# One parking transfer per pair of blocks, another order of queries, and a new plan, in a fused attention and state-space kernel

## The chip, the cores and the metric

The kernel runs on one core of a Trainium2 chip. A core has five engines that run their own instruction streams side by side and meet through semaphores: PE (matmuls), ACT (activation functions), DVE (vector operations), POOL (vector operations on SBUF) and SP, which here issues nearly all DMA transfers. SBUF is the working memory, 128 partitions wide; PSUM is the small memory into which PE writes. The metric is the device time of one execution in microseconds (us); less is better.

## What is computed

One layer has two branches over the same input x (2048 positions, 512 channels) and a gate between them. Cut to what matters:

```python
g = sigmoid((x * gate_w).sum(-1, keepdims=True))
q, k, v = split(x @ wqkv)                  # 32 heads of 16 channels
p = softmax(einsum("bhqd,bhkd->bhqk", q, k) * 16 ** -0.5)
a = einsum("bhqk,bhkd->bhqd", p, v).reshape(1, 2048, 512) @ wo
K = einsum("dn,dnl,dn->dl", C, exp(dt * A * l), dt * B).real   # 128 states
b = causal_convolution(x, K) + x * Dskip   # written with an FFT of length 4096
return g * a + (1 - g) * b
```

Nearly all the time goes to the softmax: 32 heads times 2048 x 2048 scores, each needing an exponential.

## The kernel before

**Attention.** The scores are cut into *tiles* of 128 keys by 512 queries. Four heads that lie in four strips of 32 partitions are worked on together; their four tiles for the same 128 keys are a *quad*. Sixteen quads (all 2048 keys) make a *block*: one set of four heads against 512 queries. There are 32 blocks, so 512 quads and 2048 tiles. Block `b` has the query chunk `qc = b // 8` and the head set `b % 8`; two blocks that follow each other (`b` even and odd) share a *pair* of channels and end up in one tile `ON`.

For three tiles at a time (a *group*, 683 of them) PE writes scores into one of two PSUM buffers `SC` (`qk`), and ACT turns them into exponentials in the ring `ET` (`ex`, line 1027), which has `NS` slots of one tile, and from group `NSG` on `NS2` slots, the further ones named `EX`. PE then multiplies a quad of exponentials with the values `VE` and adds them up in the PSUM buffer `OA` (`pv`), whose columns are the 512 queries of the block. All of these run through one helper, so all matmuls show as line 760.

**Quads given to DVE and POOL.** So that ACT needs fewer exponentials, some quads are taken from it. For such a quad, four groups in a row give their third tile to DVE, so that ACT does two tiles a group instead of three. DVE turns the score into an integer whose bits, read as bf16, are about the exponential (`bits`, line 1049, tile `DZ`). POOL makes three shifted copies by an integer addition over the whole quad (line 1068, tile `DU`; line 1064 is the same on DVE for the last groups), and PE multiplies all four versions with the values (`sums`), four sets of four matmuls instead of one set. The mean of the four has a small error.

**The other branch.** DVE builds powers and tables for the state-space kernel in four quarters (`bases`, `tables`: tiles `Z`, `B`, `T`), PE makes convolution taps from them (`kstage`, PSUM buffer `MB`), the taps go to HBM and come back as `H`, the input as `U`, and PE convolves them (`ystage`, 32 steps, MB<-U,H). Projections, the gate and the output product run in between, all through the one buffer `MB`.

**End of a block.** `norm_a` (line 1089) transposes `OA` in squares of 32 by 32 into `OT`, so that the queries lie on partitions; `norm_b` takes the reciprocal of the sums (1097), multiplies in the gate `gq` for `qc >= 2` (1100), and multiplies out into `ON` (1106). For the first `SPILL = 3` query chunks, `ON` of a pair is *parked* in HBM (`gm_od`, line 1823, in `norms`) and later comes back by a transposing DMA as `OnR` (line 1702, in `outs`); for the last chunk `norm_c` transposes it on the spot.

**Order of queries.** Projections place Q through `ROWS` and `TURNED` (line 861, and line 1895 for the first one): of each 128 queries, position 8 t + r holds query 16 r + t. The outputs leave for HBM in the same order (`out_dma`).

**What sets the order.** A planner in the kernel's own Python code, with a cost per instruction, writes out each engine's stream. `Sched.fill` picks pieces of side work (projections, tables, convolution, output) until the modelled time at which ACT ends a group plus `OVER` (two values: for a group with a tile on DVE, and without). `decide` chooses which quads go to DVE: it needs a free `DZ` buffer (`WIN`: group range, number of `DZ`, number of `DU`), modelled idle time on DVE (`DVCAP`), and fewer quads so far than the table `PACE` allows at that group (pairs of group and quads, straight lines between them). A quad may also lie across two blocks between the groups `STRX` and `STRE`. Where PE would otherwise have too little to do, it gets filler matmuls on a zero tile `wm`; `FILL` and `LOW` (from group 260 on) say how much. `GATE`, `BG0` to `BG3`, `XGO` say from which point on side work may start. DMA transfers with `pace` are issued only when the modelled queue of transfers is short enough (`BACK`), and follow ACT's groups through a semaphore. `LAZY`, `PDEL`, `OUTP`, `TP`, `KP` and `REST` set priorities; `US` sets the numbers of `U` buffers.

Of the kernel before, what the change touches and what calls it, by code (L numbers as in the profile page):

```python
# [12 lines left out]
ALU = mybir.AluOpType  # L13

P = 128
S = 2048
D = 512
NH = 32
DH = 16
T = 16  # L20
R8 = P // T
# [9 lines left out]
NDSEM = 56  # L31
ZCOL = .216 / 512
VLD = .0545
LAZY = 5
PDEL = 0.43
ZEND = 260
OUTP = 3.78
YSEG = 2
KSEG = 4
FILL = 1450  # L40
LOW = 1200
SURP = 192
FILL2 = 1500
OVER = (0.27, 0.64)
REST = (13, 1, 1792, 425)
DLAG = .6
PLAG = .4
TURN = dict(F=.105, R=.105, C=.105, H=.06)
# [5 lines left out]
VC = .065  # L54
ZLAG = .6
BARE = 2
NS = 20
NS2 = 24
NSG = 395
LATE = (5, 3)  # L60
XS = 128 * DH ** -.5 / math.log(2)
CUTS = (26, 56, 94)
XB = 128 * (127 - math.log2(5.3794))
WIN = ((0, 480, 2, 4), (480, 679, 4, 6))
PACE = ((0, 0), (61, 0), (78, 0.0), (149, 0.0), (206, 12.77), (270, 23.66), (340, 38.94), (414, 52.88), (500, 77.45), (564, 96.69), (630, 111.83), (683, 119.39))
DVEND = 679
YLP = 2
YQ = 0
XGO = 'g19'
YGO = 'projs'  # L70
YLGO = 'K14'
GATE = 'g100'
BG0 = 'g25'
BG1 = 'g20'
BG2 = 'K3'
BG3 = 'K3'
TP = 0.86
KP = 0.85
NB = 2
NT = 2  # L80
TB = 4
DIGITS = ("L16", "L64", "L80")
TM = (3,)
NZ = 2
US = [2, 12, 3]
HS = [4, 44, 8]
BACK = 0.66
UN4 = 4
HN = 1
UB = 1.10  # L90
# [3 lines left out]
OB = 0.49  # L94
# [7 lines left out]
WARM0 = 7  # L102
NN = 128
SPILL = 3
DVCAP = 8.7
DVK = 14
JS = ((2, 0, 3, 1), (1, 0, 2, 3), (0, 2, 1, 3))
FREE = 'u{}.2'
DVL = 16
STRX = 460  # L110
STRE = 640
STRK = (13, 14, 15)
VW = 136
VG = 4 * VW + 16
ROWS = [[P, 4], [R8, T], [1, R8]]
TURNED = [[P, 4], [1, T], [T, R8]]
ONES = struct.unpack("<f", bytes.fromhex("803f803f"))[0]


# [625 lines left out]
def record(nc, p, B, ins):  # L745
    KT, Qm, VE, ET, OT, ON, Rz = (B[n] for n in ("KT", "Qm", "VE", "ET", "OT", "ON", "Rz"))
    OnT = {3: B["OnT3"]}
    OA, MB = B["OA"], B["MB"]
    SC = [B["SC0"], B["SC1"]]
    sch = Sched(p)  # L750
    op, dma = p.op, p.dma
# [64 lines left out]
    for k in range(7):  # L816
        n = 1 << k
# [268 lines left out]

    def norm_a(b):
        w = b % 2
        op("DVE", lambda v: v.transpose(OT(512 * w, [[1, 512]]), OA(0, [[1, 512]])), [(OA, 0, b)], [(OT, w, b)], c=.64)  # L1089

    def norm_b(b, n, mul=True):
        w = b % 2 + 1 - n
        R = [(OT, x, b - b % 2 + x) for x in range(w, w + n)]
        K = range(w, w + n)
        qc = b // 8
        yield ("DVE", .3, 1)
        op("DVE", lambda v: v.reciprocal(Rz(16 * w, [[16, n], [1, 16]]), OT(512 * w + 16, [[512, n], [32, 16]])), R, [(Rz, x) for x in K], c=.22 + .02 * n, lk=False)
        if qc >= 2:
            yield ("DVE", .2, 1)
            op("DVE", lambda v: v.tensor_tensor(Rz(16 * w, [[16, n], [4, 4], [1, 4]]), Rz(16 * w, [[16, n], [4, 4], [1, 4]]),  # L1100
                                                B["gq"](4 * (qc - 2), [[0, n], [1, 4], [8, 4]]), ALU.mult),
               [(Rz, x) for x in K] + [(B["gq"], j) for j in range(4)], [(Rz, x) for x in K], c=.12)
        if not mul:
            return
        yield ("DVE", .6, 1)
        op("DVE", lambda v: v.tensor_tensor(ON(16 * w, [[16, n], [32, 16], [1, 16]]), OT(512 * w, [[512, n], [32, 16], [1, 16]]),
                                            Rz(16 * w, [[16, n], [1, 16], [0, 16]]), ALU.mult), R + [(Rz, x) for x in K], [(ON, x) for x in K], c=.07 + .27 * n)
# [518 lines left out]
    def gate():  # L1626
        gp, ge, g, g1, gwT, gl = (B[n] for n in ("gp", "ge", "g", "g1", "gwT", "gl"))
        yield ("AFTER", "V1.3")
        yield ("LOCK", "MB")
        for q4 in range(4):  # L1630
            yield ("PE", MM)
            for c in range(4):
                mm(lambda c=c: MB(0, [[1, 512]], 32 * c, 32), lambda q4=q4: gwT(32 * q4, [[1, 32]]),
                   lambda c=c, q4=q4: xT(q4 * S + 512 * c, [[1, 512]]),
                   [xk(k, q4) for k in range(4)] + [(gwT, 0), (gwT, 1)], [(MB, 0, 'gate')], q4 == 0, q4 == 3, pos=(0, 32 * c), c=MM if c == 0 else 0, a=128, cfg="C")
        yield ("DVE", .7, -1)
        op("DVE", lambda v: v.tensor_copy(gl(0, [[4, P], [1, 4]]), MB(0, [[1, P], [P, 4]])), [(MB, 0, 'gate')], key("gl"), c=.62)
        sch.unlock("MB")
        for c in range(4):
            yield ("SP", .6)  # L1640
            dma("SP", lambda e, c=c: e.dma_start(B["gld"].dram(4 * c, [[16, P], [1, 4]]), gl(0, [[4, P], [1, 4]], 32 * c, 1)), key("gl"), [(B["gld"], c)], c=.6, lat=2.5)
        yield ("SP", .6)
        dma("SP", lambda e: e.dma_start(gp(0, [[1, 16]]), B["gld"].dram(0, [[16, T], [16 * T, R8], [1, 16]])), [(B["gld"], c) for c in range(4)], key("gp"), c=.6, lat=2.5)
        yield ("AFTER", GATE)
        yield ("ACT", .3)
        op("ACT", lambda a: a.activation(ge(0, [[1, 16]]), gp(0, [[1, 16]]), AF.Exp, scale=-1.0), key("gp"), key("ge"), c=.2)  # L1646
        yield ("POOL", .4)
        op("POOL", lambda v: v.memset(B["gt"](0, [[1, NC]]), 0.0), [], [(B["gt"], j) for j in range(8)], c=.3)
        yield ("DVE", .4)
        op("DVE", lambda v: v.tensor_scalar(gp(0, [[1, 16]]), ge(0, [[1, 16]]), 1.0, None, ALU.add), key("ge"), key("gp"), c=.17)  # L1650
        op("DVE", lambda v: v.reciprocal(g(0, [[1, 16]]), gp(0, [[1, 16]])), key("gp"), key("g"), c=.25)
        op("DVE", lambda v: v.tensor_scalar(g1(0, [[1, 16]]), g(0, [[1, 16]]), -1.0, 1.0, ALU.mult, ALU.add), key("g"), key("g1"), c=.17)
        yield ("SP", .6)
        dma("SP", lambda e: e.dma_start(B["gd"].dram(0, [[16, P], [1, 16]]), g1(0, [[1, 16]])), key("g1"), [(B["gd"], 0)], c=.6, lat=2.5)
        for j in range(4):
            yield ("SP", .6)
            dma("SP", lambda e, j=j: e.dma_start(alt("gt", [[16, R8], [1, 16]], 32 * j), B["gd"].dram(0, [[16 * R8, T], [16, R8], [1, 16]])),
                [(B["gd"], 0)], [(B["gt"], j)], c=.6, lat=2.5)
            yield ("SP", .6)
            dma("SP", lambda e, j=j: e.dma_start(alt("gt", [[16, R8], [1, 8]], 32 * j + 1), B["gd"].dram(8, [[16 * R8, T], [16, R8], [1, 8]])),  # L1660
                [(B["gd"], 0)], [(B["gt"], 4 + j)], c=.6, lat=2.5)
        sch.mark("gt")
        yield ("SP", .6)
        dma("SP", lambda e: e.dma_start(B["gg"].dram(0, [[16, P], [1, 16]]), g(0, [[1, 16]])), key("g"), [(B["gg"], 0)], c=.6, lat=2.5)
        for j in range(4):
            yield ("SP", .6)
            dma("SP", lambda e, j=j: e.dma_start(B["gq"](0, [[8, 4], [1, 8]], 32 * j, 32), B["gg"].dram(8, [[16, 32], [512, 4], [1, 8]])),
                [(B["gg"], 0)], [(B["gq"], j)], c=.6, lat=2.5)
        sch.mark("gq")

    fo, Wo = B["fo"], B["Wo"]
# [18 lines left out]
    def outs():  # L1690
# [6 lines left out]
        for k in range(SPILL):  # L1697
            for pi in range(4):
                yield ("AFTER", f"od{k}.{pi}")
            for r in range(4):  # L1700
                yield ("SP", 1.35)
                dma("SP", lambda e, k=k, r=r: e.dma_start_transpose(B[f"OnR{k}"](128 * r, [[512, 4], [1, 128]]), B["od"].dram(512 * D * k + 128 * r * D, [[D, 128], [1, D]])),
                    [(B["od"], (k, pi, j)) for pi in range(4) for j in range(4)], [(B[f"OnR{k}"], r)], c=1.35, lat=3, b=1.3, pace=True)
        yield ("AFTER", "gt")
        for blk in range(NBLK):
            yield ("AFTER", f"yr{blk}")
# [28 lines left out]
    o, z, w = SC[(NG - 2) % 2], SC[(NG - 1) % 2], D // 2  # L1735
# [73 lines left out]
    def norms():  # L1809
        for b in range(31):  # L1810
            yield ("AFTER", f"ob{b}")
            yield ("DVE", .75, -2)
            norm_a(b)
            sch.mark(f"n{b}")
            if b == 30:
                yield from norm_b(b, 1)
            if b % 2 == 1:
                yield from norm_b(b, 2)
                k, pi = b // 8, (b % 8) // 2
                if k < SPILL:  # L1820
                    for j in range(4):
                        yield ("SP", .6, 3)
                        dma("SP", lambda e, k=k, pi=pi, j=j: e.dma_start(B["od"].dram(512 * D * k + P * pi + 32 * j, [[D, 32], [32 * D, 16], [1, 32]]), ON(0, [[32, 16], [1, 32]], 32 * j, 32)),
                            [(ON, 0), (ON, 1)], [(B["od"], (k, pi, j))], c=.57, lat=4, b=OB, pace=True)
                    sch.mark(f"od{k}.{pi}")
                else:
                    yield ("DVE", .7, 1)
                    norm_c(b)
# [92 lines left out]
    for g in range(NG):  # L1921
# [13 lines left out]
        if g + 1 < NG:  # L1935
# [5 lines left out]
            while lack >= 256 and bare:  # L1941
                n = 512 if lack >= 512 else 256
# [21 lines left out]
        while lack >= 256 and p.tm["PE"] < t + over and g < NG - 1:  # L1964
# [4 lines left out]
            n = 512 if lack >= 512 else 256  # L1969
# [67 lines left out]
```

## Time and profile before

| what | us |
|---|---|
| median of three runs | 746.74 (744.98 to 746.99) |
| the profiled execution | 746.18 |
| its span, first to last instruction | 744.3 |
| first exponential on ACT starts | 10.83 |
| parking transfers | 48, of 32 KB |

A profile shows one execution. Its span is a little shorter than the execution's time; what lies around it (1.9 us here) is not in the trace. The busy time of an engine is the time in which an instruction of its own ran; semaphores, branches and the issue of transfers don't count. The *chain that ended last* is followed back from the last instruction to whatever released each step. A row of a view gives line, engine, operation, output and input tiles with their shapes, the count, then the busy time and the mean in ns, then how long the engine had stood idle before such instructions and what ended it. "Issue" means that the engine waited for nothing that the profile shows.

### The profile page before, as it was taken

What the parts mean: (1) busy time and instruction counts of PE and PEld (TensorE: products, weight loads), DVE (VectorE), ACT (ScalarE), POOL (GpSimd) and SP (SyncE); (2) the same over time, 40 slices, a digit from 0 to 9 for tenths busy, and PEclk for the clock granted to TensorE, in tenths of its full rate; (3) what the DMA queues carried; (4) which work ended last, traced back from release to release, by engine and by line L of the source; (5) the groups of instructions that cost most, each with busy time, mean ns of one, the idle gap of its engine ahead of it and who ended that gap; (6) DMA issues with size and microseconds to landing.
All of it is one profiled execution on the core that took longest, in us unless ns stands there. A gap on an engine that the chain in (4) does not pass through costs nothing.

```text
span 744.3 us, 31873 instructions
## 1 busy us (share of the span) xinstructions
PE 692.2 (93%) x14173; PEld 299.0 (40%) x14173; DVE 659.3 (89%) x1109; ACT 728.8 (98%) x696; POOL 362.1 (49%) x365
## 2 busy tenths in 40 slices
PE   8888788888899999999999989999999999999997
PEld 4332333334444444444455444544443442222222
DVE  6999999999999999988999987977888888898886
ACT  7999999999999999999999989999999999999995
POOL 3000000000026465647545655577888888888783
PEclk9999999999999999999999999999999999999999
DMA  9556931324666755315789774478566741001001
GB/s 221 149 114 158 179 44 41 76 47 127 161 170 180 185 154 148 111 31 155 200 219 232 199 215 130 103 164 201 155 174 146 202 113 30 19 20 27 20 15 37
DMA packets 167182, 94.36 MB, mean 127 GB/s; under 512 B 107330, under 2 KB 148484, under 8 KB 167044
## 3 DMA queue, kind: packets, MB, share of 16 engines
q1 hardware_dynamic: 166084, 91.47, 50.0%
q8 instruction: 111, 1.82, 1.0%
q10 hardware_dynamic: 960, 0.85, 0.4%
q14 instruction: 27, 0.22, 0.1%
HBM read 63.42 MB, written 18.90 MB: 111 GB/s over the span
## 4 chain that ended last, share of the span: by engine, by line
ACT 91%; PE 8%; DVE 0%; issue 0%; DVEq 0%
ACT ET L1027 86%; ACT EX L1027 5%; PE SC L760 3%; PE OA L760 3%; PE MB L760 2%; DVE Qm L1895 0%; DVE VE L870 0%; DVE fo L1996 0%; DVEq L722 0%; DVE wm L814 0%; DVE KT L1898 0%; ACT ge L1646 0%; DVE idf L815 0%; DVEq L386 0%
## 5 line engine op out<-in xcount | busy, mean ns | idle before, releaser
L1027 ACT ACTIVATE ET<-SC 128x1024 bf16<-128x1024 f32 (+1 forms) x636 | 684.5, 1335 | 4.2 <-PE SC L760 4.0
L1068 POOL INT64_ADD DU<-DZ x345 | 354.6, 1042 | 344.5 <-PE MB L760 184.9
L1049 DVE TENSOR_SCALAR DZ<-SC 128x512 uint16<-128x512 f32 x464 | 310.6, 685 | 58.9 <-PE SC L760 54.9
L760 PE MATMUL SC<-Qm,KT 32*128 32x512 bf16 x2048 | 272.8, 386 | 10.6 <-ACT ET L1027 6.2
L760 PE MATMUL OA<-ET,VE 128*32 128x512 bf16 x1489 | 155.0, 389 | 30.6 <-ACT ET L1027 29.4
L760 PEld LDWEIGHTS SC<-Qm,KT 32*128 32x128 bf16 x2048 | 69.1, 91 | 193.7 <-ACT ET L1027 124.8
L760 PE MATMUL OA<-DU,VE 128*32 128x512 bf16 x1392 | 134.2, 387 | 0.6 <-POOL DU L1068 0.5
L760 PEld LDWEIGHTS MB<-U,H 128*32 128x32 bf16 x4096 | 91.3, 143 | 32.2 <-issue 15.6
L760 PE MATMUL MB<-U,H 128*32 128x128 bf16 (+7 forms) x4096 | 97.4, 224 | 2.0 <-issue 1.9
L760 PEld LDWEIGHTS OA<-ET,VE 128*32 128x32 bf16 x1489 | 40.0, 95 | 98.1 <-ACT ET L1027 54.1
L760 PE MATMUL OA<-wm 128*32 128x256 bf16 (+3 forms) x550 | 75.1, 343 | 1.2 <-DVE idf L815 1.2
L1121 DVE TENSOR_TENSOR T<-B,DT 128x1536 bf16<-128x1536 bf16 x64 | 59.6, 972 | 0.0
L760 PEld LDWEIGHTS OA<-DU,VE 128*32 128x32 bf16 x1392 | 35.5, 95 | 48.6 <-issue 40.3
L1027 ACT ACTIVATE EX<-SC 128x1024 bf16<-128x1024 f32 (+1 forms) x47 | 51.0, 1219 | 0.0
L760 PEld LDWEIGHTS MB<-T,Z 128*32 128x32 bf16 x2048 | 41.7, 156 | 12.2 <-issue 10.2
L760 PE MATMUL MB<-T,Z 128*32 128x64 bf16 (+1 forms) x2048 | 46.2, 236 | 0.0
L760 PE MATMUL OA<-DZ,VE 128*32 128x512 bf16 x464 | 45.8, 385 | 0.0
L1121 DVE TENSOR_TENSOR ft<-Z 128x512 f32<-128x512 f32 (+3 forms) x48 | 38.3, 820 | 0.3
L1121 DVE TENSOR_TENSOR Z<-ft,ft 128x1024 bf16<-128x1024 bf16 (+3 forms) x56 | 33.8, 604 | 0.5
L1602 DVE TENSOR_TENSOR Yst<-MB,gt 128x512 bf16<-128x512 f32 x32 | 21.8, 681 | 3.8 <-PE MB L760 3.8
L760 PEld LDWEIGHTS OA<-wm 128*32 128x32 bf16 (+2 forms) x550 | 20.8, 96 | 10.3 <-issue 7.0
L1089 DVE STREAM_TRANSPOSE OT<-OA 128x512 f32<-128x512 f32 x32 | 22.7, 710 | 2.0 <-PE OA L760 2.0
(143 smaller groups left out, 411.2 us busy)
## 6 DMA issues: line engine op xcount, KB each, us to landing
H<-gm_kd SPq DMA_DIRECT2D x128, 256.0 KB, 4.1
U<-gm_xs SPq DMA_DIRECT2D x128, 134.2 KB, 3.7
T<-B SPq DMA_DIRECT2D x16, 256.0 KB, 2.7
gm_yd<-Yst SPq DMA_DIRECT2D x16, 256.0 KB, 3.2
gm_kd<-Ks SPq DMA_DIRECT2D x64, 40.0 KB, 2.2
gm_xs<-xP SPq DMA_DIRECT2D x16, 136.0 KB, 5.8
gm_pd<-L SPq DMA_DIRECT2D x8, 256.0 KB, 4.3
Z<-gm_pd SPq DMA_DIRECT2D x8, 256.0 KB, 3.7
```

The costliest lines, as they stand in the source:

```text
L760: op("PE", lambda t: t.matmul(out(), lhsT(), rhs(), start=start, stop=stop, skip_group_check=True, **kw), R, W, c=c, lat=.15, a=a, cfg=cfg)
L1027: op("ACT", lambda a: a.activation(E(at, [[1, 512 * n]]), sc(0, [[1, 512 * n]]), AF.Exp, scale=DH ** -0.5), [(sc, i, g) for i in range(n)] ...
L1049: op("DVE", lambda v: v.tensor_scalar(z.u16(512 * k, [[1, 512]]), sc(1024, [[1, 512]]), XS, XB, ALU.mult, ALU.add), [(sc, 2, g)], [(z, k, ...
L1068: op("POOL", lambda v, u=u, cut=cut: v.int64_add(u.u64(), z.u64(), cut * 0x0001000100010001), R, [(u, 0, i)], c=1.016, lat=.09, lk=True)
L1089: op("DVE", lambda v: v.transpose(OT(512 * w, [[1, 512]]), OA(0, [[1, 512]])), [(OA, 0, b)], [(OT, w, b)], c=.64)
L1121: op(eng, lambda v: v.tensor_tensor(o(), a(), b_(), f), R, W, c=c)
L1602: op("DVE", lambda v, w=w, h=h: v.tensor_tensor(Yst(1024 * w + 4 * h, [[128, R8], [8, 16], [1, 4]]), MB(0, [[1, R8], [R8, 16], [NC, 4]]), ...
```

## The change

Parking becomes one transfer of 128 KB a pair of blocks instead of four of 32 KB. One transfer can only walk the partitions in their order, so row `16 p + a` of the parked chunk now holds what lies on partition `p` of its strip in square `a`. For this, `norm_a` reads `OA` in other steps (`BACKS`: one pattern for the parked chunks, one for the last), and the copies that place Q use other `ROWS` and `TURNED`: of each 128 queries, position 64 s + m now holds query 2 m + s. Sizes and counts of these instructions stay. The gate `gq` is stored in one order for the third chunk and in another for the fourth, and loaded with eight transfers instead of four. The transposing loads now wait for one parking transfer a pair.

Around this the planner's numbers are new; the description of the change says that two quads more go to DVE and POOL.

```diff
-LAZY = 5
-PDEL = 0.43
+LAZY = 4
+PDEL = 0.45
-OUTP = 3.78
+OUTP = 4.02
-FILL = 1450
-LOW = 1200
+FILL = 1500
+LOW = 1300
-OVER = (0.27, 0.64)
-REST = (13, 1, 1792, 425)
+OVER = (0.37, 0.82)
+REST = (12, 0, 1792, 475)
-NS = 20
+NS = 18
-NSG = 395
+NSG = 305
-WIN = ((0, 480, 2, 4), (480, 679, 4, 6))
-PACE = ((0, 0), (61, 0), (78, 0.0), (149, 0.0), (206, 12.77), (270, 23.66), (340, 38.94), (414, 52.88), (500, 77.45), (564, 96.69), (630, 111.83), (683, 119.39))
+WIN = ((0, 560, 3, 4), (560, 679, 4, 6))
+PACE = ((0, 0), (61, 0), (78, 0), (149, 0.0), (206, 12.24), (270, 23.13), (346, 36.66), (426, 58.37), (500, 81.91), (564, 97.72), (630, 116.08), (683, 123.09))
-XGO = 'g19'
+XGO = 'g34'
-BG0 = 'g25'
-BG1 = 'g20'
-BG2 = 'K3'
-BG3 = 'K3'
+BG0 = 'g20'
+BG1 = 'g0'
+BG2 = 'K4'
+BG3 = 'K6'
-KP = 0.85
+KP = 0.48
-US = [2, 12, 3]
+US = [2, 13, 3]
-BACK = 0.66
+BACK = 0.53
-DVCAP = 8.7
+DVCAP = 8.45
-STRX = 460
-STRE = 640
+STRX = 470
+STRE = 660
-ROWS = [[P, 4], [R8, T], [1, R8]]
-TURNED = [[P, 4], [1, T], [T, R8]]
+ROWS = [[P, 4], [64, 2], [1, 64]]
+TURNED = [[P, 4], [1, 2], [2, 64]]
+BACKS = ([[8, 16], [P, 4], [1, 8]], [[P, 4], [1, 8], [8, 16]])
...
-        op("DVE", lambda v: v.transpose(OT(512 * w, [[1, 512]]), OA(0, [[1, 512]])), [(OA, 0, b)], [(OT, w, b)], c=.64)
+        op("DVE", lambda v: v.transpose(OT(512 * w, [[1, 512]]), OA(0, BACKS[b // 8 >= SPILL])), [(OA, 0, b)], [(OT, w, b)], c=.64)
...
-                                                B["gq"](4 * (qc - 2), [[0, n], [1, 4], [8, 4]]), ALU.mult),
+                                                B["gq"](16 * (qc - 2), [[0, n], [1, 4], [4, 4]] if qc > 2 else [[0, n], [4, 4], [1, 4]]), ALU.mult),
...
-            dma("SP", lambda e, j=j: e.dma_start(B["gq"](0, [[8, 4], [1, 8]], 32 * j, 32), B["gg"].dram(8, [[16, 32], [512, 4], [1, 8]])),
+            dma("SP", lambda e, j=j: e.dma_start(B["gq"](0, [[1, 16]], 32 * j, 32), B["gg"].dram(8, [[1, 4], [16, P]]), allow_slow_non_contiguous=True),
+                [(B["gg"], 0)], [(B["gq"], (2, j))], c=.6, lat=2.5)
+            yield ("SP", .6)
+            dma("SP", lambda e, j=j: e.dma_start(B["gq"](16, [[4, 4], [1, 4]], 32 * j, 32), B["gg"].dram(12, [[16, 32], [512, 4], [1, 4]])),
...
-                    [(B["od"], (k, pi, j)) for pi in range(4) for j in range(4)], [(B[f"OnR{k}"], r)], c=1.35, lat=3, b=1.3, pace=True)
+                    [(B["od"], (k, pi)) for pi in range(4)], [(B[f"OnR{k}"], r)], c=1.35, lat=3, b=1.3, pace=True)
...
-                    for j in range(4):
-                        yield ("SP", .6, 3)
-                        dma("SP", lambda e, k=k, pi=pi, j=j: e.dma_start(B["od"].dram(512 * D * k + P * pi + 32 * j, [[D, 32], [32 * D, 16], [1, 32]]), ON(0, [[32, 16], [1, 32]], 32 * j, 32)),
-                            [(ON, 0), (ON, 1)], [(B["od"], (k, pi, j))], c=.57, lat=4, b=OB, pace=True)
+                    yield ("SP", .6, 3)
+                    dma("SP", lambda e, k=k, pi=pi: e.dma_start(B["od"].dram(512 * D * k + P * pi, [[32, 4], [D, 512], [1, 32]]), ON(0, [[32, 16], [1, 32]])),
+                        [(ON, 0), (ON, 1)], [(B["od"], (k, pi))], c=.6, lat=5, b=4 * OB, pace=True)
```

More of the change, by code (lines that the diff above doesn't have):

```diff
@@ L1100, in norm_b @@
             op("DVE", lambda v: v.tensor_tensor(Rz(16 * w, [[16, n], [4, 4], [1, 4]]), Rz(16 * w, [[16, n], [4, 4], [1, 4]]),
-                                                B["gq"](4 * (qc - 2), [[0, n], [1, 4], [8, 4]]), ALU.mult),
-               [(Rz, x) for x in K] + [(B["gq"], j) for j in range(4)], [(Rz, x) for x in K], c=.12)
+                                                B["gq"](16 * (qc - 2), [[0, n], [1, 4], [4, 4]] if qc > 2 else [[0, n], [4, 4], [1, 4]]), ALU.mult),
+               [(Rz, x) for x in K] + [(B["gq"], (qc, j)) for j in range(4)], [(Rz, x) for x in K], c=.12)
         if not mul:
@@ L1666, in gate @@
             yield ("SP", .6)
-            dma("SP", lambda e, j=j: e.dma_start(B["gq"](0, [[8, 4], [1, 8]], 32 * j, 32), B["gg"].dram(8, [[16, 32], [512, 4], [1, 8]])),
-                [(B["gg"], 0)], [(B["gq"], j)], c=.6, lat=2.5)
+            dma("SP", lambda e, j=j: e.dma_start(B["gq"](0, [[1, 16]], 32 * j, 32), B["gg"].dram(8, [[1, 4], [16, P]]), allow_slow_non_contiguous=True),
+                [(B["gg"], 0)], [(B["gq"], (2, j))], c=.6, lat=2.5)
+            yield ("SP", .6)
+            dma("SP", lambda e, j=j: e.dma_start(B["gq"](16, [[4, 4], [1, 4]], 32 * j, 32), B["gg"].dram(12, [[16, 32], [512, 4], [1, 4]])),
+                [(B["gg"], 0)], [(B["gq"], (3, j))], c=.6, lat=2.5)
         sch.mark("gq")
```

## The prediction

> **What bounds the kernel now.** I read the page's busy shares and its chain first, then the chain in order of time, then the windows.
>
> ```profile
> span 744.3 us, 31873 instructions
> ...
> PE 692.2 (93%) x14173; PEld 299.0 (40%) x14173; DVE 659.3 (89%) x1109; ACT 728.8 (98%) x696; POOL 362.1 (49%) x365
> ...
> ACT 91%; PE 8%; DVE 0%; issue 0%; DVEq 0%
> ```
>
> ACT is busy nearly always and carries 91% of the chain that ended last. What it does there is one kind of instruction, the exponential of two or three score tiles (the chain's longest pieces, out of its pieces in order of time: start, length, what):
>
> ```profile
> 17.34 130.41 ACT ET L1027 x97
> ...
> 549.30 9.17 ACT ET L1027 x10
> ...
> 718.95 0.55 PE OA L760 x8
> 719.49 0.37 PE SC L760 x3
> ```
>
> Early on all groups have three tiles: 130.41 / 97 = 1.344 us each. Late all have two, the third tile going to DVE: 9.17 / 10 = 0.917 us each. One tile less on ACT is thus worth 1.344 - 0.917 = 0.427 us, if ACT never waits. From 715 us on the chain runs through PE in steps of 0.55 + 0.37 = 0.92 us, the same beat: there PE and ACT are equally late.
>
> ```profile
> ACT ET L1027 <- PE SC L760: 4.0, 6, 1.7
> ```
>
> That is the row of ACT's waits for its scores: 4.0 us in six waits, the longest 1.7. Where they lie:
>
> ```profile
> 350.00:400.00 50.00, 48.45 (x1127) 24.22 (x1119) 45.95 (x73) 50.00 (x50) 28.51 (x29) 1.00 0.78 207
> 400.00:450.00 50.00, 46.98 (x1073) 22.85 (x1074) 44.39 (x65) 47.42 (x47) 27.72 (x27) 0.97 0.83 221
> 450.00:500.00 50.00, 49.40 (x1157) 24.34 (x1157) 40.33 (x67) 49.89 (x51) 30.84 (x30) 1.00 0.52 119
> 500.00:550.00 50.00, 49.39 (x1073) 23.28 (x1070) 41.72 (x70) 50.00 (x54) 38.04 (x38) 1.00 0.72 188
> ```
>
> and finer, around one place:
>
> ```profile
> 425.00:432.00 7.00, 4.59 (x157) 3.11 (x157) 4.90 (x6) 5.81 (x5) 1.92 (x2) 1.00 0.99 243
> 432.00:437.00 5.00, 5.00 (x69) 1.59 (x63) 4.06 (x6) 3.61 (x4) 2.06 (x2) 0.66 0.40 116
> ```
>
> Columns: length, busy time of PE, PEld, DVE, ACT, POOL, granted clock, DMA share, GB/s. ACT loses 50.00 - 47.42 = 2.58 us between 400 and 450, and the timeline shows the cause:
>
> ```profile
> 431.62 0.49 PE L760 MATMUL MB<-U,H 128*32 128x104 bf16 x18 [1.93 <-issue]
> ...
> 432.49 1.94 ACT L1027 ACTIVATE ET<-SC 128x1024 bf16<-128x1024 f32 x2 [1.68 <-PE SC L760]
> ```
>
> PE stood 1.93 us for "issue", so for nothing that the kernel waits on, while the DMA share was 0.99; ACT then starved 1.68 us. Afterwards the clock was low: 0.66 over 5 us, which is 0.34 x 5 / 0.5 = 3.4 us at half speed. The page's queue list shows what PE can have waited for without a semaphore:
>
> ```profile
> q8 instruction: 111, 1.82, 1.0%
> ```
>
> 111 blocks of 1.82 MB / 111 = 16.4 KB come by DMA beside the data. I read the hole as such a block of PE's own instructions held up by full DMA engines. That one hole is a matter of where transfers happen to lie, and any new plan redraws it.
>
> **The change, part by part.**
>
> *Two quads more.* The planner gives chosen key tiles ("quads": four score tiles) to DVE and POOL. Rows:
>
> ```profile
> L1068 POOL INT64_ADD DU<-DZ x345 | 354.6, 1042 | 344.5 <-PE MB L760 184.9
> L1049 DVE TENSOR_SCALAR DZ<-SC 128x512 uint16<-128x512 f32 x464 | 310.6, 685 | 58.9 <-PE SC L760 54.9
> ```
>
> 464 tiles are 116 quads. The diff holds no count; I take its words, 118, so eight tiles leave ACT: 8 x 0.427 = **3.42 us less on ACT**. The table PACE supports it: it caps the quads started by a given group, and at group 426 the cap rises from 52.88 + 12/86 x 24.57 = 56.3 to 58.37, while at group 275 it falls from 23.66 + 5/70 x 15.28 = 24.75 to 23.13 + 5/76 x 13.53 = 24.02. So quads move from early to middle, and the middle gains.
>
> What the other engines pay. DVE: 8 x 0.685 = 5.5 us, against 744.3 - 659.3 = 85 us idle. POOL: 6 x 1.04 = 6.3 us, half idle. PE: a quad takes 16 value matmuls instead of 4; in the chain's row above eight take 0.55 us, so four 0.28: 2 x 3 x 0.28 = 1.7 us. Where will they go?
>
> ```profile
> 450.00:500.00 50.00, 3.96 (x40) 1.07 (x40) 26.54 (x40) 30.84 (x30) 1.00 0.52 119
> 500.00:550.00 50.00, 4.89 (x52) 1.38 (x52) 34.44 (x53) 38.04 (x38) 1.00 0.72 188
> ```
>
> These are the windows for tile DZ alone (here PE, PEld, DVE, POOL). From 500 us nearly every group already gives a tile to DVE (53 for 54 of ACT's instructions); before it, 40 for 51. Room is only before 500, and the caps point to 350 to 500 us: at groups 275 and 423, which ACT reaches up to 10 us before these times (counting its instructions), they are 55.45 - 24.75 = 30.7 quads apart before and 57.56 - 24.02 = 33.5 after (at 423: 52.88 + 9/86 x 24.57 and 36.66 + 77/80 x 21.71). A cap is no count, but I take 2.8 more there: 2.8 x 4 x 0.685 = 7.7 us of DVE in windows where DVE idles 4.05 + 5.61 + 9.67 = 19.3 us, and 2.8 x 3 x 0.28 = 2.4 us of PE. PE's cover there is filler, matmuls on zeros (tile wm):
>
> ```profile
> 350.00:400.00 50.00, 1.75 (x24) 0.64 (x24) 0.00 (x0) 1.00 0.78 207
> 400.00:450.00 50.00, 2.76 (x40) 0.78 (x40) 0.00 (x0) 0.97 0.83 221
> 450.00:500.00 50.00, 1.40 (x20) 0.51 (x20) 0.00 (x0) 1.00 0.52 119
> ```
>
> That is 5.9 us. PE also idles 150 - 144.83 = 5.2 us in the three rows, 1.9 of them in the hole: 9.2 us of cover. Against it stand 2.4 us of new work and 2.8 x 4 x 0.427 = 4.8 us less time: 7.2. The cover holds with 2.0 us left, so PE's part is 0; without it PE sets the beat there and every us of PE work costs one.
>
> *Parking.* Four transfers of 32 KB become one of 128 KB, in runs of 64 bytes as before, so the engines carry the same packets.
>
> ```profile
> L1823 SPq DMA_DIRECT2D gm_od<-ON x48: 315/486/1102, 78.6 to 590.8; - x48
> ...
> gm_od<-ON SPq DMA_DIRECT2D x48, 32.0 KB, 2.7
> ```
>
> SP issues 36 fewer: 36 x 0.486 = 17.5 us saved if one long issue costs what a short one does, 0 if it costs as four. A landing takes between 2.7 us, as one of the four does, and 4 x 2.7 = 10.8 us. Nobody waits for either: ON is overwritten by the next pair, (590.8 - 78.6) / 11 = 47 us later on average, and SP is not on the chain. Cost 0, except that the loads queued behind it on SP move up by the 1.5 us of three issues and can crowd.
>
> *Order of queries.* The steps change in the transpose L1089 and in the two copies that place Q; counts and sizes don't.
>
> ```profile
> L1089 DVE STREAM_TRANSPOSE OT<-OA 128x512 f32<-128x512 f32 x32 | 22.7, 710 | 2.0 <-PE OA L760 2.0
> ...
> L861 DVE CAST Qs<-MB 128x512 bf16<-128x512 f32 x15 | 10.3, 689 | 0.8 <-PE MB L760 0.6
> L861 DVE CAST KT<-MB 128x512 bf16<-128x512 f32 x15 | 10.3, 686 | 0.7 <-PE MB L760 0.6
> ```
>
> Strided Qs and straight KT cost the same (689 and 686 ns), so steps out of PSUM are free there; a strided transpose has no row. Lower end 0; upper end one pass more, 32 x 0.71 = 22.7 us of DVE, inside its 85 us idle. I take 0, by Qs. The gates gq come in eight transfers instead of four, half of them element by element:
>
> ```profile
> L1100 DVE TENSOR_TENSOR Rz<-Rz,gq x9: 190/419/847, 463.6 to 737.2; 128x32 f32<-128x32 f32 x7, 128x16 f32<-128x16 f32 x2
> L1667 SPq DMA_DIRECT2D gq<-gm_gg x4: 432/432/458, 163.7 to 165.1; - x4
> ```
>
> From the issue at 165 us to the first reader at 463.6 lie 298 us, so 0.
>
> *Slack.* OVER lets PE's planned side work run past ACT's tick by 0.37 and 0.82 us instead of 0.27 and 0.64. Between nothing and 0.10 to 0.18 us a group lies the price; only six waits of ACT speak for room, so 0. FILL and LOW ask for 3% and 8% more side work a group; on 5.9 us of filler that is 0.5 us at most, within the 2.0 left. The other numbers of the plan (LAZY, BACK, BG0 to BG3, US, STRX and the like) shift work and add none: 0, their risk stands in C and D. The ring ET of 18 slots instead of 20 (24 from group 305) costs nothing while ACT waits for no slot: no such wait stands in its rows.
>
> **Sum**, against the profiled execution, 746.18 us with a span of 744.3: 746.18 - 3.42 = **742.8**. The median shown is 746.74, 0.6 higher.
>
> **Rivals.**
>
> *A, the forecast*: ACT stays the bound, holes cost about as now: 742.8.
>
> *B, the hole at 430 us is not drawn again*: 742.8 - 2.58 = 740.2. For it: ACT's longest wait is the only one of its size. Against: the DMA load stays. [...]
>
> *C, one hole more*: 742.8 + 2.58 = 745.4. [...]
>
> *D, slower: PE becomes the bound between 350 and 500 us.* Filler is nearly gone there, and side work may run longer by OVER. The side work that could move in is the convolution, 32 steps of
>
> ```profile
> L760 PE MATMUL MB<-U,H 128*32 128x128 bf16 (+7 forms) x4096 | 97.4, 224 | 2.0 <-issue 1.9
> ```
>
> 97.4 / 32 = 3.0 us each. To end over 748.4 (0.3% over 746.18) the stretch must lose 5.6 us, so 5.6 + 2.0 of cover = 7.6 us must move in: three steps, 9.1 us, do it, and give 742.8 + 9.1 - 2.0 = 749.9. Against: from 500 to 550 us PE is busy 49.39 of 50 and ACT loses nothing.
>
> *E, no tile more leaves ACT* (the plan misses its two quads): 746.2.
>
> **How the numbers follow.** Chances: A 0.40, B 0.18, C 0.18, D 0.18, E 0.06. A measurement of this kernel can tell about 0.3%, 2.2 us, from no change: faster (A, B) 0.58, within (C, E) 0.24, slower (D) 0.18. Likeliest 742.8. The range leaves out D alone, 0.18: from B's 740.2, less half of the 1.8 us by which the lowest run shown (744.98) lies under their median, 739.3, to 748.4, where D begins.
>
> **What would show it.** 472 DZ tiles and 12 parking issues; two-tile groups up by 8; ACT's beats 1.344 and 0.917 unchanged; ACT's waits for scores near 4 us (A), 1.4 (B) or 6.6 (C), many small ones between 350 and 500 us (D); the strided transpose near 710 ns. Wrong if DZ stays 464, if the steps of the convolution crowd into 350 to 500 us, or if parking lies in the timeline just ahead of a PE stall.

## The result and the profile after

The changed kernel takes **755.37 us** (median of 6 runs, 754.03 to 759.34); the kernel before, timed beside it, 746.3 us. One of the six runs of the kernel before took 833.7 us, in a slow state, and the ratio leaves it out. The ratio is 1.0133 with a 95% interval of 1.0102 to 1.0163: 1.3% slower, where 742.8 us was forecast. The profiled execution of the changed kernel took 754.03 us, its span 752.2, which is 7.9 more than the 744.3 before.

The page of the changed kernel, the lines that answer to those of before:

```profile
span 752.2 us, 31836 instructions
...
PE 691.8 (92%) x14165; PEld 299.7 (40%) x14165; DVE 663.9 (88%) x1117; ACT 728.2 (97%) x696; POOL 369.3 (49%) x371
...
ACT 73%; PE 19%; DVE 4%; DMA 3%; issue 1%; DVEq 0%; SPq 0%
...
L1069 POOL INT64_ADD DU<-DZ x351 | 361.7, 1047 | 304.8 <-DVE B L1322 149.3
L1050 DVE TENSOR_SCALAR DZ<-SC 128x512 uint16<-128x512 f32 x472 | 314.8, 685 | 54.0 <-PE SC L761 51.1
```

The two quads came: 472 tiles DZ instead of 464, POOL six instructions more. DVE is busier by 4.6 us and POOL by 7.2, as the two quads ask; PE and ACT are not. Yet ACT's share of the chain that ended last falls from 91% to 73%, and **DMA, at nothing before, holds 3%**. (Most of ACT's fall comes with the new plan: e1_four below, which loses no time, stands at 78%.) The waits tell more. ACT's, in the changed kernel:

```profile
ACT ET L1028 <- PE SC L761: 10.2, 12, 2.1
...
ACT ET L1028 <- PE OA L761: 1.9, 2, 1.5
```

10.2 + 1.9 = 12.1 us stand where 4.0 stood (e1_four below has 3.4 + 1.8). PE's, in the same kernel:

```profile
PE MB L761 <- DMA H<-gm_kd: 2.4, 3, 1.3
PE MB L761 <- DMA T<-B: 2.0, 1, 2.0
PE MB L761 <- issue: 1.4, 1, 1.4
```

PE waits for loads of the other branch: H, the taps of the convolution, and T, from which taps are made. In the chain in order of time (start, length, what) two pieces are loads H:

```profile
294.20 7.27 DMA H<-gm_kd
...
560.91 4.77 DMA H<-gm_kd
```

What lies ahead of the second is in SP's timeline of the changed kernel (start, length, line, what SP issued):

```profile
554.20 0.51 SPq L1620 DMA_DIRECT2D Yl<-gm_yd  x1
554.75 0.61 SPq L1826 DMA_DIRECT2D gm_od<-ON  x1
555.76 4.46 SPq L1571 DMA_DIRECT2D H<-gm_kd  x1
560.26 0.60 SPq L1614 DMA_DIRECT2D gm_yd<-Yst  x1
```

The parking itself is issued in 0.61 us. **The issue behind it, a load of H that takes about 0.55 us elsewhere, takes 4.46 us.** The load of the chain's second piece is issued only behind these, at 560.91. For the load issued at 555.76 the list of transfers in the window from 555 to 557 us gives the time from issue to landing, 7.6 us:

```profile
H<-gm_kd SPq DMA_DIRECT2D x1, 256.0 KB, 7.6
```

555.76 + 7.6 = 563.36, and that is where the timeline of all engines has PE again, and ACT after it:

```profile
563.36 0.45 PE L761 MATMUL MB<-U,H 128*32 128x128 bf16 x16 [1.26 <-DMA H<-gm_kd]
564.18 1.94 ACT L1028 ACTIVATE ET<-SC 128x1024 bf16<-128x1024 f32 x2 [1.16 <-PE SC L761]
```

The parking at 292.75 us does the same: the next issue takes 4.4 us and its H lands after 7.3, at 301.5, where PE has waited 0.98. Of the twelve next issues in the changed kernel ten take between 2.5 and 7.7 us; the other two come late. Before, the four short issues took 2.0 to 3.0 us together and the next one 0.3 to 0.7, once 2.2 (a transposing load).

The row of the parking shows none of this. For the changed kernel, by tile:

```profile
L1826 SPq DMA_DIRECT2D gm_od<-ON x12: 601/614/642, 78.3 to 599.7; - x12
L1706 SPq DMA_TRANSPOSE OnR<-gm_od x12: 1200/1267/2187, 583.1 to 628.6; - x12
...
DMA to landing us min/median/max: 3.2/4.5/4.8
```

Issue 0.61 us: harmless by itself. The landings in this view are those of the transposing loads OnR alone; it has none for the parkings. But the trace also keeps a mark for every step of the semaphore that tells of a transfer's end. By the last of these marks the parkings of the changed kernel land 7.6 to 8.6 us after their issue, the first one 10.1; those of the kernel before landed after 1.7 to 5.1.

### The profile page after: what moved, and what is told of

Read it like the earlier page. It is cut to its first block, busy times and chain, and to the rows that moved or that the text cites. A ratio compares the mean times of both kernels' runs of the same rounds, so it can differ in the third digit from the quotient of the medians.

```text
span 752.2 us, 31836 instructions
## 1 busy us (share of the span) xinstructions
PE 691.8 (92%) x14165; PEld 299.7 (40%) x14165; DVE 663.9 (88%) x1117; ACT 728.2 (97%) x696; POOL 369.3 (49%) x371
## 4 chain that ended last, share of the span: by engine, by line
ACT 73%; PE 19%; DVE 4%; DMA 3%; issue 1%; DVEq 0%; SPq 0%
ACT ET L1028 64%; ACT EX L1028 9%; PE OA L761 7%; PE SC L761 7%; PE MB L761 4%; DMA H<-gm_kd 2%; DVE DZ L1050 1%; DMA gm_xs<-xP 1%; DMA T<-B 1%; DVE T L1122 0%; DVE OT L1090 0%; DVE Yst L1603 0%; DVE ft L1122 0%; DVE OnT L1114 0%; DVE Rz L1101 0%
## 5 line engine op out<-in xcount | busy, mean ns | idle before, releaser
L1028 ACT ACTIVATE ET<-SC 128x1024 bf16<-128x1024 f32 (+1 forms) x591 | 637.8, 1254 | 12.2 <-PE SC L761 10.2
L1069 POOL INT64_ADD DU<-DZ x351 | 361.7, 1047 | 304.8 <-DVE B L1322 149.3
L1050 DVE TENSOR_SCALAR DZ<-SC 128x512 uint16<-128x512 f32 x472 | 314.8, 685 | 54.0 <-PE SC L761 51.1
L761 PE MATMUL OA<-ET,VE 128*32 128x512 bf16 x1384 | 144.1, 391 | 32.5 <-ACT ET L1028 31.3
L761 PE MATMUL OA<-DU,VE 128*32 128x512 bf16 x1416 | 136.9, 389 | 0.1
L761 PE MATMUL MB<-U,H 128*32 128x104 bf16 (+7 forms) x4096 | 98.6, 224 | 3.9 <-DMA H<-gm_kd 2.4
L1028 ACT ACTIVATE EX<-SC 128x1024 bf16<-128x1024 f32 (+1 forms) x92 | 94.3, 1140 | 0.6 <-PE SC L761 0.5
L761 PE MATMUL OA<-wm 128*32 128x512 bf16 (+3 forms) x490 | 71.0, 345 | 1.2 <-DVE idf L816 1.2
L761 PE MATMUL OA<-EX,VE 128*32 128x512 bf16 x192 | 32.4, 386 | 0.9 <-ACT EX L1028 0.8
```

The costliest lines, as they stand in the source:

```text
L761: op("PE", lambda t: t.matmul(out(), lhsT(), rhs(), start=start, stop=stop, skip_group_check=True, **kw), R, W, c=c, lat=.15, a=a, cfg=cfg)
L1028: op("ACT", lambda a: a.activation(E(at, [[1, 512 * n]]), sc(0, [[1, 512 * n]]), AF.Exp, scale=DH ** -0.5), [(sc, i, g) for i in range(n)] ...
L1050: op("DVE", lambda v: v.tensor_scalar(z.u16(512 * k, [[1, 512]]), sc(1024, [[1, 512]]), XS, XB, ALU.mult, ALU.add), [(sc, 2, g)], [(z, k, ...
L1069: op("POOL", lambda v, u=u, cut=cut: v.int64_add(u.u64(), z.u64(), cut * 0x0001000100010001), R, [(u, 0, i)], c=1.016, lat=.09, lk=True)
```

## The experiments

**Theory 1.** The change writes the parked block with an HBM pattern whose outermost step has 4 positions, [[32, 4], [D, 512], [1, 32]]; before, each transfer had 32 outermost. I assume that this step sets how many DMA engines carry a transfer. Then the 2048 packets of 64 bytes go through four engines, and what SP issues next waits. **Theory 2**: one transfer of 128 KB is too long in itself. **Theory 3**: the new plan costs it, the parking is innocent.

*e1_four*: the changed kernel and its plan, with four transfers again; the order on PE, DVE, ACT and POOL is that of the changed kernel.

```diff
-dma("SP", ... B["od"].dram(512 * D * k + P * pi, [[32, 4], [D, 512], [1, 32]]), ON(0, [[32, 16], [1, 32]])
+for j in range(4):
+    dma("SP", ... B["od"].dram(512 * D * k + P * pi + 32 * j, [[16 * D, 32], [D, 16], [1, 32]]), ON(0, [[32, 16], [1, 32]], 32 * j, 32)
```

> The new kernel with its plan, order of queries and gate loads, but each pair parked in four transfers of 32 partitions again; PE, DVE, ACT and POOL run the same instructions in the same order as in the new kernel. Theory 1 (few engines: the one transfer, whose outermost dimension has 4 steps, runs on 4 of the 16 DMA engines, so its 2048 packets take 5.3 us instead of about 2.5 and SP's next issue is held up to 5 us): no issue behind a parking over 2 us, the PE waits on DMA H and T at 301, 563 and 214 us are gone, 743 to 749 us. Theory 2 (size: 2048 packets in one transfer are too many for what takes SP's issues, whatever the layout): the same here. Theory 3 (the new plan itself loses, by the thinner margins of OVER and a crowded stretch, and the parking is beside the point): 752 to 756 us.

*e2_parkonly*: the kernel before with its own plan numbers, and of the change only the parking in one transfer, the order of queries that it needs and the gates gq.

> The old kernel with its old plan, and only the one parking transfer, the order of queries and the gate loads of the change; the four compute engines run the old kernel's instructions in its order. Theories 1 and 2: SP's next issue is held 4 to 5 us after a parking wherever it comes within that time, loads of H, U and T come late, 748 to 754 us. Theory 3: within 1.5 us of the old kernel, 745 to 748 us.

*e3_one16*: the changed kernel, one transfer of the same 2048 packets, other addresses.

```diff
-B["od"].dram(512 * D * k + P * pi, [[32, 4], [D, 512], [1, 32]])
+B["od"].dram(512 * D * k + 256 * D * (pi // 2) + 32 * (pi % 2), [[2 * D, P], [64, 16], [1, 32]])
```

> The new kernel with one parking transfer a pair of the same 2048 packets of 64 bytes, but to addresses whose outermost dimension is the 128 partitions (2 rows apart) instead of 4 strips; the parked data lie in another order in HBM, so the output of the first three query chunks is permuted. Theory 1: packets spread over all engines, 2 to 3 us, next issue under 2 us, and the time of the four-transfer kernel within 2 us. Theory 2: next issue held 4 to 5 us as in the new kernel, 754 to 757 us. Theory 3: 752 to 756 us.

*e4_two*: the changed kernel, two transfers of 64 partitions each, outermost step 2.

```diff
+for j in range(2):
+    dma("SP", ... B["od"].dram(512 * D * k + P * pi + 64 * j, [[32, 2], [D, 512], [1, 32]]), ON(0, [[32, 16], [1, 32]], 64 * j, 64)
```

> The new kernel with two parking transfers a pair, of 64 partitions and 1024 packets each, whose outermost dimension has 2 steps. Theory 1: two engines for each transfer, and if they are the same two, 2048 / 2 x 10.5 ns = 10.8 us of packets a pair, the next issue held up to 10 us, slower than the new kernel: 757 to 775 us. Theory 2: halves are easier than the whole, next issue held 2 to 3 us, 747 to 754 us. Theory 3: 752 to 756 us.

Measured: e1_four 746.4 us, ratio 1.0014 (1.0 within the interval 0.9991 to 1.0038); e2_parkonly 753.92, 1.0106 (1.0048 to 1.0164); e3_one16 746.01, 1.0016 (0.9987 to 1.0044); e4_two 818.28, 1.097 (1.0898 to 1.1042).

Theory 3 falls: with one transfer as the change writes it the old plan is 1.1% slower as well, and with four the new plan is at the time of before. Theory 2 falls: e3_one16 moves the same bytes in one transfer and loses nothing. Nor is it a matter of addresses: e1_four writes the same addresses in the same order within each 32 partitions as the change, and e4_two does so too. In e3_one16 the load H behind the parking at 548.66 us, the same load as above, lands after

```profile
H<-gm_kd SPq DMA_DIRECT2D x1, 256.0 KB, 4.2
```

4.2 us instead of 7.6. Two other issues behind a parking in e3_one16 took 3.3 and 3.5 us, where under 2 was expected. Theory 1 also gave the sign of the least expected case: e4_two has twice the transfers of the change and half the size, and is 63 us slower than it. The size it missed: 757 to 775 us was expected. Its SP timeline:

```profile
316.70 5.57 SPq L1827 DMA_DIRECT2D gm_od<-ON  x2
322.38 6.56 SPq L1571 DMA_DIRECT2D H<-gm_kd  x2
```

and two rows of PE's waits in it:

```profile
PE MB L761 <- DMA H<-gm_kd: 42.9, 6, 14.9
...
PE MB L761 <- DMA T<-B: 10.9, 3, 4.9
```

Now the second parking of a pair is held by the first, and the load by both.

*e8_eight and e9_long4* give the dose between, and tell the number of engines from the number of packets. Edits of the changed kernel:

```diff
 e8_eight
+B["od"].dram(512 * D * k + 256 * D * (pi // 2) + 32 * (pi % 2), [[64, 8], [D, 256], [1, 32]]), ON(0, [[32, 16], [1, 32]])
 e9_long4
+B["od"].dram(512 * D * k + 256 * D * (pi // 2) + P * D * (pi % 2), [[P, 4], [D, P], [1, P]]), ON(0, [[1, 512]])
```

> The changed kernel, parking in one transfer, its 2048 packets of 64 bytes laid out so that the outermost step of the HBM side is 8 (4 in the change, 16 or more in e3_one16): the three parked query chunks come out in another order. Theory (a transfer runs on as many DMA engines as its outermost step allows, and SP's next issue is held until their rings have room): eight engines carry 256 packets each instead of 512, the last packet lands near 3 us after the first instead of 5.5, SP's next issue is held 1 to 2.5 us instead of 4 to 5, and the kernel takes 746 to 749 us. Rival (the outermost step acts as a switch, all 16 engines or a slow path): 754 to 756 us like the change.

> The changed kernel, parking in one transfer whose outermost step on the HBM side is 4 as in the change, but the same 128 KB laid out in 512 runs of 256 bytes instead of 2048 of 64: the three parked query chunks come out in another order. Question: is it four engines as such, or the number of small packets that each of them gets? Theory P (packets: in the change 512 packets for each engine take 5.2 us, so 10 ns each, and SP's next issue is held while they drain): 128 packets for each engine, 10 to 20 ns each, are through in 1.3 to 2.6 us, the next issue is held under 2.5 us as in e8_eight, and the time is 745 to 748 us. Rival B (bytes: 32 KB through one engine take as long in any run length): 5 us, next issue held 4 to 5 us, 754 to 756 us.

Measured: e8_eight 745.26 us, just under the range expected, 1.0002 (0.9982 to 1.0022); e9_long4 746.3, 0.9982 (0.9961 to 1.0004). SP's timeline in e8_eight:

```profile
343.17 0.68 SPq L1826 DMA_DIRECT2D gm_od<-ON  x1
343.89 2.40 SPq L1614 DMA_DIRECT2D gm_yd<-Yst  x1
```

and in e9_long4:

```profile
469.08 0.60 SPq L1826 DMA_DIRECT2D gm_od<-ON  x1
469.73 0.92 SPq L1614 DMA_DIRECT2D gm_yd<-Yst  x1
```

All five together. The drain is the time over which a parking's packets start, in the trace's packet records, from the shortest to the longest of the parkings that have no other transfer of such packets beside them; the number of engines is my reading of the semaphore's marks, told below the table, and the packets on each are 2048 (512 in e9_long4) divided by it:

| kernel | engines | packets on each | drain, us | next issue, us | time, us | ratio |
|---|---|---|---|---|---|---|
| e3_one16 | 16 | 128 of 64 bytes | 1.3 to 3.2 | 0.3 to 1.4, two of 3.3 and 3.5 | 746.01 | 1.0016 |
| e8_eight | 8 | 256 of 64 bytes | 2.4 to 3.2 | 2.0 to 2.4 when it follows at once | 745.26 | 1.0002 |
| e9_long4 | 4 | 128 of 256 bytes | 1.9 to 2.4 | 0.8 to 1.8 when it follows at once | 746.3 | 0.9982 |
| the change | 4 | 512 of 64 bytes | 5.2 to 6.0 | 4.0 to 5.7 when it follows within 1.5 us | 755.37 | 1.0133 |
| e4_two | 2, twice | 1024 of 64 bytes | 11.2 to 11.8, both | 5.8 to 6.0, the pair itself 5.4 to 6.6 | 818.28 | 1.097 |

(The parking at 78 us is left out of the column of next issues: a transposing load follows it, 3.7 to 7.7 us long.) The trace names no engine, but it keeps a mark for every step of a transfer's semaphore, and these can be counted: 16 for each parking of e3_one16 and of the kernel before, 9 in e8_eight, 5 in the change and in e9_long4, 3 in e4_two. Where it is not 16, one mark comes about 1 us after the issue (later for the second of a pair in e4_two) and the others at the end, so 8, 4, 4 and 2 of them. I read each of these, and each of the 16, as one engine: that is the count in the table, and it equals the outermost step at 8, 4, 4 and 2. The shortest drains go with it too, at the four patterns with packets of 64 bytes: 1.29 / 128, 2.39 / 256, 5.2 / 512 and 11.2 / 1024 come to 10.1, 9.3, 10.2 and 10.9 ns a packet on each engine (an estimate; the last if the pair of e4_two shares its two engines). So theory 1 stands with its assumption as far as marks and drains bear it. What costs is a long drain, by this reading packets times their time on an engine, not four engines as such: e9_long4 has the five marks of the change, drains in 1.9 to 2.4 us and loses nothing. And holds of up to 2.4 us (in e3_one16 two of 3.3 and 3.5) cost this kernel nothing that can be measured, those of 4 to 5.7 us cost 9 us in all, and two in a row, of about 5 and 6 us, cost 72.

**How the hold becomes 9 us.** With the same order on the compute engines, the time that ACT's groups take over their steady steps (1.329 us for three tiles, 0.903 for two, added up from the starts of all 683) is 26.1 us in the changed kernel and 17.5 in e3_one16. The two waits for H shown above (and what follows within 3 us) make 0.7 + 1.9 us of the 8.6. The rest lies in holes at 126 us (1.5 us, none in e3_one16), 216 to 218 (2.9 against 1.0), 290 to 295 (2.9 against 1.4) and 399 to 403 (2.4 against 1.4). The first two stand behind late transfers too (gm_xs, T); for the other two, and for how much of each is the parking's, no cause is shown. Two of the holes appear without four engines as well: e1_four loses 3.0 us at the groups of the third, and e8_eight 1.9 us at that of the first, in an execution of 748.93 us against its median of 745.26. So the runs show that the layout of the parking costs the 9 us; the path of each of them, beyond the 2.6 us at the waits for H, stays open.

**Second question: what became of the two quads?** With eight tiles off ACT, e1_four should be 3.4 us faster than before and isn't. By the same sum ACT loses 18.1 us over its steps in it, 14.3 before: 3.8 more. As much, 3.8 us, lies at eight groups that lose 0.2 us or more here and in e3_one16 alike, so they belong to the plan. Its page:

```profile
ACT 78%; PE 16%; DVE 4%; DMA 1%; issue 0%; DVEq 0%
```

PE and DVE hold 20% of the chain that ended last, where they held 8%. Theory M: the wider margin OVER lets side work stand ahead of the next scores. Three runs move that number alone. *e5_margins* is e1_four with

```diff
-OVER = (0.37, 0.82)
+OVER = (0.27, 0.64)
```

> The changed kernel with four parking transfers (as e1_four), and the planner's margin OVER put back from (0.37, 0.82) to (0.27, 0.64) us; the plan's other numbers stay the changed ones. Question: e1_four gives eight tiles off ACT (3.4 us) and is no faster than before. Theory M (margins): the wider margin lets side work on TensorE stand ahead of the next scores, and ACT then waits in many small holes; these eight places above 0.2 us cost 3.8 us in e1_four. Then this kernel has fewer of them, 1 us or less in sum over those of the kernel before, and runs 2 to 3.5 us under the kernel before. Rival N (any new plan draws its own holes, the margin has no part in them): ACT's time over its beats stays 17 to 20 us as in e1_four (18.1), at other groups, and the time is within 1.5 us of e1_four.

*e6_before_margins* is the kernel before with the opposite edit, *e7_margin_one* is e1_four with (0.27, 0.82):

> The kernel before with OVER widened from (0.27, 0.64) to (0.37, 0.82) us and nothing else; the plan that follows from it is a new one. Theory M: small holes appear that the kernel before doesn't have, ACT's time over its beats rises from 14.3 us by 2 to 4 us, and the kernel is 2 to 4 us slower than before. Rival N: a new draw, within 1.5 us of before or off it by one hole of 2.6 us to either side.

> As e5_margins, but only the first of the two margins is put back, 0.37 to 0.27 us (that for groups whose next one gives a tile to DVE); the order of ACT's instructions is then that of e1_four, instruction for instruction, and only TensorE's and DVE's orders differ. Theory M: the small holes at groups before a two-tile group go, so the time lies between e1_four and e5_margins, about 1.5 us under e1_four. Rival N: within 1.5 us of e1_four, the holes at other groups.

Measured: e5_margins 756.52 us, 1.0142 (1.0124 to 1.0161); e6_before_margins 751.8, 1.0089 (1.0064 to 1.0114); e7_margin_one 754.8, 1.0121 (1.0099 to 1.0143). Theory M falls: back at the old margin the new plan is about 10 us slower, not faster. The rival's "within 1.5 us of e1_four" falls too. ACT's waits in e7_margin_one show where it went:

```profile
ACT fo L2003 <- remote: 13.8, 1, 13.8
ACT ET L1028 <- PE SC L761: 5.0, 7, 2.5
```

ACT runs the same instructions in the same order as in e1_four and is done 1 us later; but then it waits 13.8 us for the last output tile, where it waited

```profile
ACT fo L2003 <- PE MB L761: 3.3, 1, 3.3
```

in e1_four (3.7 before). The chain of e7_margin_one alternates there between the output projection on PE and the sums on DVE, 2.2 us a round:

```profile
741.17 1.29 PE MB L761 x20
...
742.55 0.70 DVE fo L1733
...
743.39 1.29 PE MB L761 x20
```

With the narrower margin the side work didn't get done while ACT ran, and was left over for the end. In e5_margins (468 tiles DZ) the same wait is 8.0 us. So in this plan **the margin is the room in which side work gets done**. That the small holes of ACT are its price is not shown: with the narrower margin ACT's losses over its steps are 19 us in e7_margin_one and 21 in e5_margins, no less than the 18.1 of e1_four. In e6_before_margins they are 20.0 us, in 32 holes above 0.2 us instead of 11, and four tiles fewer leave ACT (460); there the wider margin does what theory M said of it, at 6 us where 2 to 4 were expected.

*e10_told* asks whether a plan that knows of the hold could avoid it: e2_parkonly with

```diff
-c=2.28, lat=4
+c=5.0, lat=6
```

> As e2_parkonly (the numbers of the plan before, parking in one transfer on four engines), but the planner is told that a parking occupies SP for 5.0 us and lands after 6 us, where e2_parkonly told it 2.28 and 4. It then plans the loads behind it 5 us later or ahead of it. Theory: the loss of e2_parkonly (7.5 to 9 us) is loads that come later than planned, so a plan that knows of the 5 us gets most of it back: 746 to 750 us, no wait of TensorE for H or U over 1 us. Rival (the slow transfer costs by itself, or the plan has no room for 12 x 5 us of SP): 752 to 756 us as in e2_parkonly.

Measured: 755.45 us, 1.0103 (1.007 to 1.0136), so no better than e2_parkonly. Its SP timeline still has

```profile
193.92 0.62 SPq L1825 DMA_DIRECT2D gm_od<-ON  x1
194.59 6.14 SPq L1508 DMA_DIRECT2D gm_kd<-Ks  x2
```

and PE's waits for H fall from 6.7 us in e2_parkonly to 1.5, while others grow (ACT's wait for the last output tile from 3.7 to 7.1 us, and 4.0 us for OA where e2_parkonly has none; the execution profiled, 760.39 us, is the longest of the six). A plan drawn anew differs in too much for this one run to say whether the hold or the plan costs the 8 us: that stays open.

No version beat the kernel before by what can be measured: e1_four, e3_one16, e8_eight and e9_long4 are level with it.

## Why the prediction was wrong, point by point

- **The step that failed: parking, "so the engines carry the same packets", "Nobody waits for either", "Cost 0".** The packets are the same; by the marks (5 for a parking, 16 for each of the four before) the number of engines that carry them isn't. I looked at the size of a run (64 bytes both times) and at who waits for the landing, not at the outermost step of the pattern, 4 against 32. My bounds for the landing, 2.7 to 10.8 us, held (7.6 to 8.6, once 10.1), and it is true that nobody waits for it: what waits is the next transfer on SP. I put "the loads queued behind it on SP move up by the 1.5 us" as its one risk; they went the other way, H at 555 us landing 7.6 us after its issue, 4.2 in e3_one16. The term was 0, it measured 8 to 9 us: a ratio to the kernel before of 1.0133 against 1.0014 in e1_four, and 1.0106 in e2_parkonly.
- "SP is not on the chain": true of before, and no argument. The loads that SP issues are one wait away from PE, and PE from ACT.
- **Two quads more, -3.42 us**: the count was right (472, and 8 groups fewer with three tiles, 210 against 218), the worth was not. The trace of e1_four gives 3.8 us back in small holes, and the measured gain is nothing (1.0014, at best 0.9991). My cover sum for PE between 350 and 500 us was not refuted there; but I counted only the quads' value matmuls as their price, and no place for the side work.
- **OVER at 0**: not so. Widened in the kernel before it costs 6 us (e6_before_margins, a plan drawn anew), and taken out of the new plan about 10 (e5_margins).
- Rival D (PE becomes the bound by crowded convolution steps, 749.9 us) had the sign and the wrong mechanism: at the groups between 350 and 500 us ACT's holes above 0.2 us add up to 3.1 us, where they were 3.5. The last condition that I named for being wrong, a parking just ahead of a PE stall, is what came.
- The strided transpose at 0: right. By tile in the changed kernel:

```profile
L1090 DVE STREAM_TRANSPOSE OT<-OA x32: 696/707/920, 43.0 to 744.4; 128x512 f32<-128x512 f32 x32
```

The median is 707 ns against 706 before, the mean 715 against 710. gq in eight transfers, the ring of 18 slots, FILL and LOW: no wait in the traces names them.
- Rivals B and C: the hole of 430 us was not drawn again there; another "issue" stall, 1.43 us, stands at 397 us. Beside both stalls the packet records have a 16 KB block of the instruction queue (429.1 to 430.2 us before, 395.6 to 396.8 now), but not whose it was. Neither decided.

## What to carry to other kernels

When transfers are merged, compare the outermost step of the pattern in HBM before and after, and read how long the packets drain: here 2048 packets of 64 bytes took 1.3 to 3.2 us with 128 positions outermost, 5.2 to 6.0 with 4, and bytes and run length stayed as they were while the queue behind slowed down. Read the price of a transfer from the issue that comes next on its queue (here 4.0 to 5.7 us), not from its own row (0.61). And tiles taken off the bound engine are worth their time only if the engines beside it still have room for everything else that must be done before the end.

## What the runs showed that I had not expected

- SP's issue of a transfer is held while an earlier one drains: 0.6 us for the parking, then 4.0 to 5.7 us for whatever follows within 1.5 us, loads and stores alike. Why it is held (a full queue, or the full rings of e8_eight's theory, are readings) no run here shows.
- The granted clock falls to 0.50, for 3.41 us, behind some short stalls of PE; what makes it fall behind one and not behind another is not shown. In the windows of the changed kernel (the last three numbers are granted clock, DMA share and GB/s), right behind the wait of 2.04 us for T:

```profile
211.00:214.50 3.50, 1.00 (x15) 0.22 (x12) 3.34 (x14) 3.31 (x3) 0.00 (x0) 1.00 1.07 223
214.80:218.20 3.40, 3.40 (x104) 1.66 (x103) 0.51 (x1) 1.46 (x1) 0.00 (x0) 0.50 0.56 147
```

The trace's clock records have three more such stretches of 3.41 us ahead of the end, from 13.5, 289.9 and 399.2 us, the last behind the "issue" stall of 1.43 us; behind the waits for H of 0.98 us at 301 and 1.26 us at 563 there is none. So a load that was 2 us late was paid twice here: ACT's steps lost 2.4 us at the wait and 0.6 at the next group, at half speed.
